# Retention and low-rank mixer kernel: queries four tokens to a partition, a reordered start, u^T of the first group by matmul, first y2 over w2 blocks

## The chip, the cores and the metric

One core of one Trainium2 chip. The metric is the device time of one execution in microseconds, as the median of several executions. Kernels that were timed together ran on the same chip, in turns with the kernel before.

## The reference

```python
# q, k, v: [8, 8, 576, 64] fp32 (batch, heads, tokens, head size)
scores = q @ k^T / 8
x = (scores * gamma_h ** (i - j) for i >= j, else 0) @ v     # retention, gamma_h = 1 - 2 ** (-5 - h)
x = x as [8, 576, 512]
u = x + (x^T @ U @ V)^T          # U: [576, 32], V: [32, 576]: mixes tokens
out = u + relu(u @ w_ch1) @ w_ch2  # 512 -> 2048 -> 512
```

## The kernel before

Two batches make a pair of 9 chunks of 128 tokens; chunk 4 ("X") holds the last 64 tokens of one batch and the first 64 of the other. The work goes in 8 groups (one per batch, of 4 or 5 chunks). A *front* computes attention and mixer of a group: k and q are transposed, `psc` are the scores, `ret` the masked scores, `po` the attention output, `xt` its scaled form, `psa`/`a_sb` the product with U, `ph` the product with V, `ut` = u, `uT` = u transposed. The MLP of a group is y1 = relu(u w1), then y2 = y1 w2, then `o_sb` = y2 + u, which is stored. While group g's MLP runs on PE, group g+1's front is woven in between, and group g+2 is loaded.

```python
    def load_chunk(p, c):                    # one token to a partition, 256 B runs
        t = qkv_pool.tile([P, 3, H, D], BF16, tag="qkv", name="qkv")
        f = stage.tile([P, 3, H, D], FP32, tag="stage", name="stage_t")
        for j, dram in ((1, k), (0, q), (2, v)):
            for rows, b, t0 in parts(p, c):
                nc.sync.dma_start(out=f[rows, j, :, :],
                    in_=dram[b, :, t0:t0 + L, :].rearrange("h s d -> s h d"))
        # ... casts; v is scaled on gpsimd

        def T(c):                            # q and k of a chunk in one transpose
            if not pe_transpose:
                nc.sync.dma_start_transpose(
                    out=qkT, in_=t[:, 0:2, :, :].rearrange("p j h d -> p (j h d)"))
                return                       # (the first group: on PE)

        def MT(c):
            if not pe_transpose:
                nc.sync.dma_start_transpose(out=dst, in_=st["u", c])
                return

        def Y2(i, f0):
            # ... 16 matmuls over f into one PSUM tile, then:
                nc.vector.tensor_tensor(out=o_sb, in0=ps, in1=st["u", c0 + i], op=ALU.add)
                nc.sync.dma_start(
                    out=out_flat[row0 + i * P:row0 + (i + 1) * P, :], in_=o_sb)

    # ...
        for c in A_CH:                       # chunks 0 to 4 of the first pair
            load_chunk(0, c)
            if c == 1:
                load_mixer()
            if c == 3:
                load_w1([0])
        interleave([], front_items(0, [], True, 0))
        load_w1(range(1, dff // W1B))
        load_w2()
        for a in chunks_of(1):
            load_chunk(*a)
        for g in range(2 * NP):
            main = mlp_items(g // 2, g % 2, sts[g // 2])
            fill = front_items(g + 1, chunks_of(g + 2)) if g + 1 < 2 * NP else []
            interleave(main, fill, 0.35 if g == 0 else 0.05, 0.9)
```

All transposes by DMA, all loads of q, k, v and all stores are issued by SyncE (SP) in this order of the program; `w1`, `w2`, U and V are loaded from GpSimd (POOL).

## Time and profile before

| | before |
|---|---|
| time, median (range) | 382.49 us (377.34 to 382.87) |
| span of the profiled run, granted clock | 381.3 us, 0.978 |
| PE busy | 329.2 us, 86% |
| first y1 matmul of groups 0, 1, 2 | 41.8, 93.0, 142.9 us |
| output store, issue to landing | 2.2 us |
| uT transpose, issue to landing | 2.5 us |

The page of the profile: busy time of each engine, then digits for 40 equal slices of the span (9 is 90% or more).

```profile
span 381.3 us, 5987 instructions
PE 329.2 (86%) x2440; PEld 176.1 (46%) x2440; DVE 142.9 (37%) x199; ACT 123.2 (32%) x244; POOL 62.4 (16%) x86
PE   2655794887997999999998989998999999999995
PEclk9999996799899999999999999999999999999999
```

The line `PEclk` is the clock that PE was granted, in tenths of full speed. After the first quarter PE is busy nearly all the time. What is left to win is at the start. A group boundary is the other place to watch. Here is the one between groups 2 and 3, SP's queue and then PE, with start, duration, what, and in brackets how long the engine had been idle and for what.

```profile
175.32 0.39 SPq L444 DMA_DIRECT2D out_dram<-o_sb  x1
175.77 2.54 SPq L390 DMA_TRANSPOSE uT<-ut  x2
178.99 0.34 SPq L444 DMA_DIRECT2D out_dram<-o_sb  x1
179.39 2.66 SPq L214 DMA_TRANSPOSE qkT<-qkv  x2
```

The busy time by stretches, during the last group, where nothing else moves data. The columns are the stretch, its length, the busy us of PE, of its weight loads (PEld), of DVE, ACT and POOL (each with its number of instructions), the granted clock, the DMA share (the mean busy share of the 16 DMA engines) and GB/s.

```profile
365.00:366.00 1.00, 1.00 (x6) 0.47 (x5) 0.00 (x0) 0.00 (x0) 0.00 (x0) 1.00 0.67 262
366.00:367.00 1.00, 1.00 (x7) 0.41 (x6) 0.02 (x1) 0.00 (x0) 0.00 (x0) 1.00 0.00 0
```

The last store is issued 3.2 us before the span ends.

### The profile page before, as it was taken

How to read it: one execution, taken by the hardware profiler on the slowest of the kernel's cores; microseconds unless marked ns; L12 is line 12 of the kernel's file. 1: busy time of each engine (PE TensorE's matmuls, PEld its weight loads, DVE VectorE, ACT ScalarE, POOL GpSimd, SP SyncE). 2: the span in 40 equal slices, each digit the busy share in tenths (PEclk: the TensorE clock that was granted, in tenths of full speed). 3: DMA queues.
4: the chain of work that ended last, by engine and by line, in shares of the span. 5: the costliest groups of instructions: out<-in, count | busy, mean ns of one | idle time of the engine just before them, and what ended most of it. 6: DMA issues, size and time to landing. Idle time of an engine off the chain costs nothing.

```text
span 381.3 us, 5987 instructions
## 1 busy us (share of the span) xinstructions
PE 329.2 (86%) x2440; PEld 176.1 (46%) x2440; DVE 142.9 (37%) x199; ACT 123.2 (32%) x244; POOL 62.4 (16%) x86
## 2 busy tenths in 40 slices
PE   2655794887997999999998989998999999999995
PEld 1432341433673444544664435444764445447642
DVE  4454201555252342544335324552544424340021
ACT  3322361200572006501771035303660056007600
POOL 2746821221022000121021001220121000000000
PEclk9999996799899999999999999999999999999999
DMA  9999999995995149995994279997991480040012
GB/s 181 206 210 179 199 196 186 206 185 132 191 212 97 57 110 194 202 211 136 175 228 83 73 126 218 186 173 157 218 196 40 114 153 2 28 125 29 0 57 83
DMA packets 173659, 54.81 MB, mean 144 GB/s; under 512 B 164864, under 2 KB 169024, under 8 KB 173632
## 3 DMA queue, kind: packets, MB, share of 16 engines
q1 hardware_dynamic: 167840, 50.09, 73.6%
q0 software_dynamic: 5792, 4.34, 7.5%
q8 instruction: 19, 0.31, 0.4%
q14 instruction: 8, 0.07, 0.1%
HBM read 37.00 MB, written 9.44 MB: 122 GB/s over the span
## 4 chain that ended last, share of the span: by engine, by line
PE 56%; DMA 18%; SPq 13%; DVE 6%; issue 3%; ACT 2%; POOL 1%; DVEq 0%; POOLq 0%
DMA stage_t<-in_q_dram 8%; SPq L190 7%; DMA uT<-ut 4%; SPq L214 4%; DMA stage_t<-in_v_dram 3%; DVE ret L281 3%; PE po L294 2%; PE psc L254 2%; PE psa L361 2%; PE ph L379 1%; SPq L390 1%; DVE o_sb L443 1%; DVE qkv L194 1%; DMA qkT<-qkv 1%; DMA U_A<-in_moe_U_dram 1%
## 5 line engine op out<-in xcount | busy, mean ns | idle before, releaser
L426 PEld LDWEIGHTS <-w_sb 128*128 128x128 bf16 x768 | 72.2, 100 | 55.9 <-issue 17.3
L195 POOL TENSOR_TENSOR qkv<-stage_t,vscale 128x512 bf16<-128x512 f32 x36 | 38.1, 1060 | 216.2 <-DMA stage_t<-in_v_dram 156.0
L281 DVE TENSOR_TENSOR ret<-psc,tri 128x1024 bf16<-128x1024 f32 x32 | 39.1, 1223 | 50.9 <-PE psc L254 50.9
L194 DVE CAST qkv<-stage_t 128x1024 bf16<-128x1024 f32 x36 | 25.8, 718 | 64.4 <-DMA stage_t<-in_q_dram 64.4
L300 DVE TENSOR_TENSOR xt<-po,qscale 128x512 bf16<-128x512 f32 x36 | 24.8, 689 | 17.6 <-PE po L294 17.5
L366 ACT ACTIVATE a_sb<-psa 128x512 bf16<-128x512 f32 x8 | 4.8, 597 | 80.5 <-PE psa L361 76.5
L385 DVE TENSOR_TENSOR ut<-ph,xt 128x512 bf16<-128x512 f32 x36 | 24.6, 689 | 14.5 <-PE ph L379 14.4
L294 PE MATMUL po<-qkv,ret 128*128 128x64 bf16 x288 | 15.6, 201 | 9.6 <-DVE ret L281 9.6
L254 PE MATMUL psc<-qkT 64*128 64x128 bf16 x288 | 16.0, 238 | 8.8 <-DMA qkT<-qkv 5.7
L294 PEld LDWEIGHTS <-ret 128*128 128x128 bf16 x288 | 13.5, 103 | 19.6 <-DVE ret L281 15.1
L244 ACT ACTIVATE s_sb<-pss 128x512 bf16<-128x512 f32 x32 | 19.0, 593 | 5.4 <-PE pss L237 5.4
L254 PEld LDWEIGHTS <-qkT 64*128 64x128 bf16 x288 | 9.1, 102 | 22.3 <-issue 10.1
L237 PEld LDWEIGHTS <-qkv 128*128 128x128 bf16 x128 | 10.5, 105 | 6.9 <-issue 1.9
L237 PE MATMUL pss<-qkv 128*128 128x128 bf16 x112 | 12.0, 235 | 1.8 <-ACT s_sb L244 1.0
L437 PEld LDWEIGHTS <-y_3686 128*128 128x128 bf16 x80 | 7.8, 98 | 9.3
L437 PEld LDWEIGHTS <-y_929 128*128 128x128 bf16 x80 | 7.8, 101 | 9.3 <-issue 1.1
L437 PEld LDWEIGHTS <-y_1861 128*128 128x128 bf16 x80 | 7.6, 98 | 8.6
L437 PEld LDWEIGHTS <-y_2793 128*128 128x128 bf16 x80 | 7.6, 98 | 8.6
L221 PE MATMUL pst<-ident,qkv 128*128 128x128 bf16 x40 | 5.2, 311 | 7.3 <-DVE qkv L194 7.3
L226 ACT ACTIVATE qkT<-pst 128x1024 bf16<-128x1024 bf16 x5 | 5.1, 1024 | 15.1 <-PE pst L221 15.1
L163 POOL DMA_DIRECT2D w_sb<-in_moe_w_ch_dram x16 | 9.3, 597 | 3.5 <-DMA w_sb<-in_moe_w_ch_dram 3.5
L437 PEld LDWEIGHTS <-y_1457 128*128 128x128 bf16 x64 | 6.1, 98 | 7.1
(522 smaller groups left out, 536.7 us busy)
## 6 DMA issues: line engine op xcount, KB each, us to landing
out_dram<-o_sb SPq DMA_DIRECT2D x36, 256.0 KB, 2.2
stage_t<-in_k_dram SPq DMA_DIRECT2D x32, 256.0 KB, 3.9
stage_t<-in_q_dram SPq DMA_DIRECT2D x32, 256.0 KB, 5.1
stage_t<-in_v_dram SPq DMA_DIRECT2D x32, 256.0 KB, 5.1
w_sb<-in_moe_w_ch_dram POOLq DMA_DIRECT2D x16, 128.0 KB, 7.2
w_sb<-in_moe_w_ch_dram POOLq DMA_DIRECT2D x8, 256.0 KB, 11.5
stage_t<-in_k_dram SPq DMA_DIRECT2D x8, 128.0 KB, 4.8
stage_t<-in_q_dram SPq DMA_DIRECT2D x8, 128.0 KB, 4.8
```

What stands on the lines that cost most here:

```text
L190: nc.sync.dma_start(out=f[rows, j, :, :], in_=dram[b, :, t0:t0 + L, :].rearrange("h s d -> s h d"),)
L194: nc.vector.tensor_copy(out=t[:, 0:2, :, :], in_=f[:, 0:2, :, :])
L195: nc.gpsimd.tensor_tensor(out=t[:, 2, :, :], in0=f[:, 2, :, :], in1=vscale[:, c, :, None].to_broadcast([P, H, D]), op=ALU.mult,)
L237: nc.tensor.matmul(pss[:, hp, :], t[:, 1, 2 * hp:2 * hp + 2, :].rearrange("p h d -> p (h d)"), vt[:, 2 * hp:2 * hp + 2, :].rearrange("p h ...
L244: nc.scalar.activation(out=s_sb, in_=pss, func=AF.Copy)
L254: nc.tensor.matmul(psc[:, hl, hp, :], qkT[pb:pb + HALF, NHP + hp, :], qkT[pb:pb + HALF, hp, :], start=True, stop=True,)
L281: nc.vector.tensor_tensor(out=ret.rearrange("p (hp hl) i -> p hl hp i", hl=2), in0=psc, in1=mask[:, None, None, :].to_broadcast([P, 2, NHP ...
L294: nc.tensor.matmul(po[:, hl, hp * D:(hp + 1) * D], ret[:, h, :], t[:, 2, h, :], start=(c == 0 and hp == 0), stop=True, skip_group_check=True,)
L300: nc.vector.tensor_tensor(out=xt.rearrange("p (hp hl d) -> p hl hp d", hl=2, d=D), in0=po[:, :, 0:NHP * D].rearrange("p hl (hp d) -> p hl ...
L385: nc.vector.tensor_tensor(out=ut, in0=ph, in1=st["x", c], op=ALU.add)
L426: nc.tensor.matmul(ps[:, 0:n], w1_sb[:, cc, f * P:(f + 1) * P], uT[:, cc, t0:t0 + n], start=(cc == 0), stop=(cc == NCC - 1),)
L437: nc.tensor.matmul(ps, st["y1"][:, f, i * P:(i + 1) * P], w2_sb[:, f, :], start=(f == 0), stop=(f == NF - 1),)
```

## The change

Its intent: (1) load q in 1 KB runs instead of 256 B, by putting four neighbouring tokens of a head into one partition. The transpose of such a tile gives the tokens of a chunk in permuted order, partition j*32+p holding token 4p+j; the mask, the scales, U, V and the output rows are permuted to match. (2) Give the start an order: batch 0, then w1, then batch 1, then w2, each waiting for the one before. (3) The first group's u^T straight from x and a_sb by matmul, without u. (4) Group 0's y2 over w2 blocks as they land, three chunks at a time. Group 1's front is transposed on PE as well.

```diff
 def load_q(g, quick=False):
+    i = nc.sync.dma_start(out=f,
+        in_=q[g, :, t0:t0 + 4 * P, :].rearrange("h (p j) d -> p h j d", j=J))   # J = 4
 ...
-    nc.sync.dma_start_transpose(out=qkT, in_=<q and k of one chunk>)
+    for m in range(4):                                  # TQ: all four chunks of q
+        nc.sync.dma_start_transpose(
+            out=qT[:, m].rearrange("p hp (j i) -> p (hp j) i", j=J),
+            in_=t[m * PJ:(m + 1) * PJ].rearrange("p hp j hl d -> p (hp j hl d)"))
+    nc.sync.dma_start_transpose(out=kT, in_=<k of one chunk>)    # TK
 ...
 def load_mixer():
+    for t, t0, m0 in ((U_A, 0, 0), (U_B, HALF, 1)):
+        for j in range(J):                              # 11 small loads in place of 6 (8 here)
+            nc.gpsimd.dma_start(out=t[j * PJ:(j + 1) * PJ, m0:m0 + 4, 0:R], in_=src[j])
+    ... put_v(V_A, 0, 0)                                # V rows permuted by a DVE copy
 ...
 Y2:
-    nc.sync.dma_start(out=out_flat[row0 + i * P:row0 + (i + 1) * P, :], in_=o_sb)
+    nc.sync.dma_start(out=dst.rearrange("(p j) d -> j p d", j=J), in_=o_sb)
 ...
+    load_x(0, 0)
+    w1_last = load_w1()
+    first = first_front()                               # u^T = x^T + (V^T a)^T in PSUM
+    i = load_q(1)
+    tc.add_manual_dep(i.ins, w1_last.ins.name, SYNC)    # batch 1 after w1
+    ... load_w2() after two chunks of batch 1 ...
+            if g == 0:
+                fill = [MH of group 0] + Front(1, True).items([], x_alone=True)
+                interleave(mlp.y1_items(), fill, 0.3, 1.2)
+                i = load_q(2)
+                tc.add_manual_dep(i.ins, w2_last.ins.name, SYNC)
+                ...
+                for f in range(NF):
+                    for i in range(3):
+                        mlp.Y2(i, f, 1)
+                mlp.Y2(3, 0, NF)
+                continue
```

## The prediction

> What bounds it now. PE is busy 329 of 381 us (busy table), and from 120 us on 18.3 to 19.4 of each 20 us (busy time by stretches): the later groups are bound by PE. The loss is at the start: the timeline has the first y1 matmul at 41.8 us and the second group's y1 at 93.0; the 288 us after that lose about 13 us to short waits (uT transposes 0.6 to 1.9 us each, waits view). Between 41.8 and 93, PE stands 4.65 us for a transpose stuck behind loads and then runs cold (630 ns a matmul against 379). DMA moves 180 to 210 GB/s, nearly all packets under 512 B: batches 0 and 1, w1 and w2 compete.
>
> What the change does.
> 1. Queries, a third of the loads, in 1 KB runs (256 B before). The Trainium skill, "DMA: Bandwidth & Descriptors", Specifications, gives 512 B as the least for line rate; at the trace's 190 GB/s for 256 B runs a group's q (1 MB) takes 5.5 us, now an estimated 3.5.
> 2. Batch 0 alone, then w1 (issued after the last V scaling, about 21 us, landed by about 34), then batch 1, then w2.
> 3. First front: per chunk about 3.8 us in place of 4.7 (0.6 less each in transposes and copy); u^T in one piece replaces four 1.8 us rounds of ph, ut, pu, uT. Against it: twelve small mixer loads on POOL (0.55 us each) before the second V scaling, and V rows copied by DVE ahead of the second mask. First y1 at 36 to 39 us.
> 4. Group 1's front is transposed on PE, with a tail of five rounds (1.5 to 1.8 us) that y1 no longer fills, then 64 y2 matmuls (13.8 us). Second y1: about 88 us, 5 earlier; the second group gains 3 more, having no uT wait.
> 5. Later groups: four q transposes and one of k before the first scores; before, one. An issue takes SP 1.2 us (128x512) or 1.25 (128x1024), landing 2.5 after. They start after the previous group's last output, about 0.5 us after y1 starts; the scores stand 3.5 to 3.9 us into PE's order. Landing after 6 to 9 us: a wait of 2 to 5 us in groups 2 to 6.
> 6. Outputs have 4 as slowest dimension. The same page ("Why a DMA increments its semaphore by 16") would put them on 4 engines: 256 KB in an estimated 2.4 us, delaying uT transposes behind them by about 1 us and the tail by 1 to 2. The trace has 2.2 us to landing now.
>
> Sum: -8 (start), -3 (second group), +1 to +5 in each of five groups, +1.5 (tail): 376 to 398. If transposes of 32 partitions issue faster, or the start gains more, it is a gain of 10 to 20. I settle at 382.
>
> Predicted: 382 us, 8 in 10 between 362 and 402; faster by over 2% 0.35, within 2% 0.32, slower by over 2% 0.33.
>
> Signs. First y1 at 36 to 39 us (step 3 too pessimistic if under 32); second y1 at 84 to 91. Waits view: PE at a group's first psc for DMA kT or qT, 2 to 5 us (none: step 5 wrong). uT waits above 1.9 us, outputs landing after more than 2.2 us (step 6). q landing in well under twice a k load's time per byte (step 1).
>
> What would make it wrong: q's transposes being cheap; front 1 hidden better behind y1; four-engine outputs holding up loads.

## More of the kernel before

```profile
178.07 0.71 PE L426 MATMUL ps_y_1862<-uT,w_sb 128*128 128x320 bf16 x4
179.72 0.70 PE L426 MATMUL ps_y_1868<-uT,w_sb 128*128 128x320 bf16 x4 [0.94 <-DMA uT<-ut]
182.80 0.40 PE L254 MATMUL psc<-qkT 64*128 64x128 bf16 x8
```

(`SPq` is SP's queue, and the duration of its lines is the time that SP took to issue; `x2` means two in a row; `DMA_DIRECT2D` is a plain copy by DMA.) SP alternates stores, uT transposes of the group that is about to start, and the q and k transposes of the first two chunks of the front after it. PE waits 0.94 us for the last uT, and not at all for the scores (`psc`), which stand some 3 us further on in its order.

## The result, and the profile after

The changed kernel is right and takes 449.26 us median (448.0 to 452.81, 4 runs) against 381.66 us for the kernel before. Ratio 1.181, 95% interval 1.169 to 1.193. (Ratios here are the mean time of one kernel's fast runs over that of the other's fast runs of the same rounds, so they are not quite the ratio of the medians quoted.)

| | before | after |
|---|---|---|
| span, granted clock | 381.3 us, 0.978 | 448.1 us, 0.914 |
| first y1 of group 0 | 41.8 | 41.6 |
| of group 1 | 93.0 | 100.4 |
| of group 2 | 142.9 | 158.3 |
| from there to the end | 238.4 | 289.8 |

So the loss of 66.8 us is 7.4 us in the start, 8.0 us in group 1, and 51.4 us in groups 2 to 7. The page of the profile after:

```profile
span 448.1 us, 6172 instructions
PE 350.1 (78%) x2486; PEld 188.1 (42%) x2520; DVE 157.6 (35%) x249; ACT 129.6 (29%) x257; POOL 66.4 (15%) x103
PE   2357787797789669985999569974999489959993
PEclk9999999598899979997799888996899979997997
```

PE has a hole at each group boundary, and its clock is below full after each hole. The same boundary as above, between groups 2 and 3, SP and then PE:

```profile
196.47 0.54 SPq L607 DMA_DIRECT2D out_dram<-o_sb  x1
197.06 4.01 SPq L504 DMA_TRANSPOSE uT<-ut  x2
201.17 0.54 SPq L607 DMA_DIRECT2D out_dram<-o_sb  x1
201.80 7.35 SPq L318 DMA_TRANSPOSE qT<-q_bf  x4
209.20 1.26 SPq L342 DMA_TRANSPOSE kT<-kv  x1
```

```profile
199.03 0.72 PE L581 MATMUL ps_y_2039<-uT,w_sb 128*128 128x320 bf16 x4
204.12 1.23 PE L581 MATMUL ps_y_2045<-uT,w_sb 128*128 128x320 bf16 x4 [4.37 <-DMA uT<-ut]
211.74 0.61 PE L403 MATMUL psc<-qT,kT 64*128 64x128 bf16 x8 [2.88 <-DMA kT<-kv]
```

Two uT transposes take SP 4.01 us where they took 2.54; the last uT comes 4.37 us late where it was 0.94; then four transposes of q take 7.35 us, and the scores wait 2.88 us more. After the first wait the first three y1 sets take 1.23 us for four matmuls against 0.71 before it: PE is at half clock. The Trainium skill, "TensorE: Matmul & The Clock Gate", Part 1, says that the clock falls to half when PE is idle and takes about 3.4 us of work to come back. The trace agrees the first time, and not in length the second. In stretches of 1 us the granted clock is 0.50 from 205 to 207 us and back at 1.00 at 208, some 3.4 us after PE began again at 204.1; after the second wait it is 0.50 from 211 to 217, and comes back in the stretch after, some 6 us after PE began again at 211.7.

Some of the waits of PE over the whole run (who waited for whom: total us, times, longest), first of before, then of after; the other lines, some as long, are left out:

```profile
PE po L294 <- DVE ret L281: 9.6, 10, 2.6
PE psc L254 <- DMA qkT<-qkv: 5.7, 2, 4.6
PE ps_y_936 L426 <- DMA uT<-ut: 1.9, 1, 1.9
PE ps_y_2800 L426 <- DMA uT<-ut: 1.6, 1, 1.6
```

```profile
PE psc L403 <- DMA kT<-kv: 14.3, 6, 3.3
PE po L440 <- DVE ret L428: 10.1, 7, 3.9
PE ps_y_2575 L581 <- DMA uT<-ut: 6.6, 1, 6.6
PE ps_y_3523 L581 <- DMA uT<-ut: 6.6, 1, 6.6
PE ps_y_3899 L581 <- DMA uT<-ut: 5.2, 1, 5.2
```

In all, the uT tile's own view gives 8.1 us in 8 waits before and 32.5 us in 6 waits after.

What are the transposes behind? After group 0's y2, three stores are issued at once, with the loads long done. The chain of waits and the busy time by stretches of the changed kernel:

```profile
96.95 6.31 DMA out_dram<-o_sb
103.39 0.70 DVE o_sb L599
```

```profile
102.00:103.00 1.00, 0.00 (x0) 0.00 (x0) 0.00 (x0) 0.15 (x1) 0.00 (x0) 1.00 0.27 104
103.00:104.00 1.00, 0.00 (x0) 0.00 (x0) 0.61 (x1) 0.00 (x0) 0.00 (x0) 1.00 0.26 100
```

The chain lists 6.31 us for the stores, and the next `o_sb`, for which only three buffers exist, is made after that; the first columns of the stretches show PE doing nothing. The DMA share stands at about a quarter at 100 GB/s: 4 of 16 engines work. That agrees with the Trainium skill, "DMA: Bandwidth & Descriptors", "Why a DMA increments its semaphore by 16 and not by 1", which says that a transfer uses the largest number of engines up to 16 that divides the slowest dimension of both sides. The changed store has `j` (4) as slowest dimension. How long one such store moves data is seen best at the end, where it is alone: the last one moves from 443.0 to 446.5 us, 3.5 us in place of 0.9. From its issue to the end of the span it is 7.0 us, where it was 3.2.

### The profile page after: what moved, and what is told of

Read it like the earlier page. It is cut to its first block, busy times and chain, and to the rows that moved or that the text cites. A ratio compares the mean times of both kernels' runs of the same rounds, so it can differ in the third digit from the quotient of the medians.

```text
span 448.1 us, 6172 instructions
## 1 busy us (share of the span) xinstructions
PE 350.1 (78%) x2486; PEld 188.1 (42%) x2520; DVE 157.6 (35%) x249; ACT 129.6 (29%) x257; POOL 66.4 (15%) x103
## 4 chain that ended last, share of the span: by engine, by line
PE 58%; DMA 14%; SPq 14%; DVE 7%; issue 2%; ACT 2%; POOL 1%; DVEq 0%; POOLq 0%
SPq L318 8%; SPq L504 4%; DMA kv_f<-in_k_dram 3%; DMA q_f<-in_q_dram 3%; DMA kT<-kv 3%; PE psc L403 2%; PE po L440 2%; DMA uT<-ut 2%; PE psa L469 2%; PE ph L486 2%; DMA out_dram<-o_sb 1%; DVE ret L428 1%; DMA kv_f<-in_v_dram 1%; DVE ut L492 1%; DVE o_sb L599 1%
## 5 line engine op out<-in xcount | busy, mean ns | idle before, releaser
L581 PEld LDWEIGHTS <-w_sb 128*128 128x128 bf16 x768 | 77.9, 108 | 93.3 <-issue 29.5
L244 POOL TENSOR_TENSOR kv<-kv_f,vscale 128x512 bf16<-128x512 f32 x32 | 33.5, 1051 | 252.6 <-DMA kv_f<-in_v_dram 162.5
L448 DVE TENSOR_TENSOR xt<-po,qscale 128x512 bf16<-128x512 f32 (+1 forms) x37 | 25.5, 690 | 24.1 <-PE po L440 24.0
L403 PE MATMUL psc<-qT,kT 64*128 64x128 bf16 x256 | 14.0, 235 | 14.8 <-DMA kT<-kv 14.3
L440 PE MATMUL po<-kv,ret 128*128 128x64 bf16 x256 | 14.1, 202 | 8.8 <-DVE ret L428 8.8
L259 DVE CAST kv<-kv_f 128x512 bf16<-128x512 f32 x32 | 15.3, 482 | 12.2 <-DMA kv_f<-in_k_dram 10.9
L403 PEld LDWEIGHTS <-kT 64*128 64x128 bf16 x256 | 7.9, 100 | 25.3 <-DMA kT<-kv 17.2
L382 PE MATMUL pss<-kv 128*128 128x128 bf16 x112 | 12.1, 236 | 6.9 <-POOL kv L244 6.8
L238 DVE CAST q_bf<-q_f 128x512 bf16<-128x512 f32 x30 | 11.6, 450 | 13.6 <-DMA q_f<-in_q_dram 13.6
L382 PEld LDWEIGHTS <-kv 128*128 128x128 bf16 x112 | 9.4, 108 | 10.9 <-issue 7.7
```

The source lines that it names most:

```text
L244: nc.gpsimd.tensor_tensor(out=dst[rows], in0=src[rows], in1=vscale[rows, c, :, None].to_broadcast([n, H, D]), op=ALU.mult,)
L382: nc.tensor.matmul(pss[:, hp, :], pair_cols(st["k", c], hp), pair_cols(vt, hp), start=(first and hp == 0), stop=True, skip_group_check=True,)
L403: nc.tensor.matmul(psc[0:n, hl, hp, 0:n], kT[pb:pb + HALF, hp, 0:n], qTv[pb:pb + HALF, hp, 0:n], start=True, stop=True,)
L440: nc.tensor.matmul(po[0:n, hl, hp * D:(hp + 1) * D], ret[:, h, 0:n], vt[:, h, :], start=((c == 0 or not cross) and hp == 0), stop=True, sk ...
L448: nc.vector.tensor_tensor(out=st["x", c][rows].rearrange("p (hp hl d) -> p hl hp d", hl=2, d=D), in0=po[rows, :, 0:NHP * D].rearrange("p h ...
L581: nc.tensor.matmul(ps[:, 0:n], w1_sb[:, cc, f * P:(f + 1) * P], uT[:, cc, t0:t0 + n], start=(cc == 0), stop=(cc == NCC - 1),)
```

## The experiments

At each boundary two things of the change come together: the stores run on four engines, and the q transposes of the next front stand behind the last store. The first theory (A) was that the stores are the main cost; the rival (B), that it is the late, fourfold q transposes; a third (C), that the new start and the new order of work cost something by themselves. The first six variants start from the changed kernel, then three from the kernel before, and the last four build a better version. Times are medians, given with the kernel before on the same chip.

### e1: stores on 16 engines

```diff
-    nc.sync.dma_start(out=dst.rearrange("(p j) d -> j p d", j=J), in_=o_sb)
+    nc.sync.dma_start(out=dst, in_=o_sb)
```

The rows come out in the wrong order: only the address pattern differs.

> Outputs written in plain row order (wrong rows on purpose, same bytes, 2 KB runs), nothing else changed: the output's slowest dimension is 128 again and not 4. Theory A (outputs run on 4 of 16 engines, about 100 GB/s, and the uT and qT transposes queue behind them): DMA share while outputs run is no longer capped at 0.25, uT waits at group starts fall from 4.4 to 6.6 us back to 1 to 2, the 4 qT issues fall from 7.7 to about 5 us; time 395 to 412 us from 449. Rival B (the five transposes before the first scores are the cost, whatever the outputs do): uT waits stay, time 435 us or more.

Measured: 418.42 us against 380.33 (ratio 1.097, 1.090 to 1.104). The signs of A came, but not its time of 395 to 412 us: more remains than A had room for. A stretch of 1 us in which three stores are out at once, and the waits of PE for transposes:

```profile
99.00:100.00 1.00, 1.00 (x6) 0.48 (x5) 0.29 (x1) 0.00 (x0) 0.00 (x0) 1.00 1.00 369
```

```profile
PE psc L403 <- DMA kT<-kv: 26.0, 7, 5.5
PE ps_y L581 <- DMA uT<-ut: 5.3, 6, 1.4
```

The same data leave at 369 GB/s, with all engines at work (share 1.00), and the uT waits are as small as before the change. But the wait for the scores' transposes has grown from 14.3 to 26.0 us: what the uT no longer lose, the q transposes do. So the stores cost 31 us net here, and a second loss was hidden behind the first.

### e2: q transposes ahead of the stores

```diff
+    def ahead(self): self.TQ(); self.TK(5 * self.par)   # q, first k of the front after next,
+    # called in the middle of the front before it, not at its start
-    add(0, self.TQ); add(0, self.TK, main[0])           # at the start of a front
```

> The four q transposes and the first k transpose of the next front are issued one group earlier (ahead of the MA stage of the front before), outputs still on 4 engines. Theory A: the waits for kT at the first psc (31 us PE and PE-load together) go, but the uT waits of 4 to 7 us stay or grow; 425 to 440 us. Rival B: most of the loss goes; 395 to 415 us.

Measured: 451.06 us against 380.33 (1.186, 1.179 to 1.192), result correct. No gain at all, against 10 to 25 us expected. PE's waits for transposes are now one line:

```profile
PE ps_y L588 <- DMA uT<-ut: 51.4, 8, 11.7
```

The wait for kT is gone, as intended, and the wait for uT has grown from 32.5 to 51.4 us. Part of that is the edit's own: the five transposes moved ahead now stand before the uT transposes in SP's queue, between the stores, and with fast stores (e10 against e1) the same move raises the wait for uT from 5.3 to 11.8 us. While the stores crawl, it matters little which transpose stands behind them.

### e4: plain stores, plain q, new start

```diff
-    load_q: one load of 1 KB runs; U, V, mask permuted; stores permuted
+    f[:, m] <- q[g, :, t0 + m*P : +P, :].rearrange("h s d -> s h d")   # 4 loads; U, V, mask, stores plain
```

The new start, the order of loads, u^T by matmul and the late q transposes (four of 128 x 512) stay.

> The query layout undone (one token to a partition, 256 B runs, plain outputs, plain U and V loads); DMA order, first u^T by matmul, first y2 over w2 blocks and four separate q transposes of 128x512 stay. If the layout alone (through its outputs) made the loss in later groups: groups 2 to 7 as in before plus the wait for five transposes, in all 395 to 415 us. If the new start and order are to blame for more than about 15 us: over 415 us. If q in 1 KB runs is worth something, the start is 2 to 4 us later than in the changed kernel.

Measured: 416.06 us against 380.33 (1.094, 1.090 to 1.098), result correct. That is about e1 again (418), a little slower than expected, with the same line of waits, 26.0 us in 7 for kT. So 1 KB loads of q, the eleven mixer loads and the V copies, taken together, cost and gain next to nothing over the whole run; what remains in e1 is theory B and possibly C. By its expectation 416 lies just in the branch that blames the new start for more than 15 us; e7 below shows that it is mostly B. The first y1 came at 35.7 us in place of 41.6, and still the second came at 100.3: the six microseconds gained in the first front did not pass on.

### e8: the same permuted rows in four stores of 32 partitions

```diff
-    nc.sync.dma_start(out=dst.rearrange("(p j) d -> j p d", j=J), in_=o_sb)
+    rows = dst.rearrange("(p j) d -> j p d", j=J)
+    for j in range(J):
+        nc.sync.dma_start(out=rows[j], in_=o_sb[j * PJ:(j + 1) * PJ])
```

> Right results: each permuted output in four DMAs of 32 partitions, whose slowest dimension is 32 on both sides. Theory A: all 16 engines work, as the run with plain outputs but with 4 issues of about 0.35 to 0.5 us where one was: 400 to 418 us. If a small DMA of 32 partitions still goes to few engines, little is gained: 430 us or more.

Measured: 434.01 us against 380.33 (1.142, 1.138 to 1.146), result correct. A repair of less than the expected size; 434 lies in the branch that was written for stores that still go to few engines, so it has to be seen which it is. The busy time in the stores' stretch, and SP's queue:

```profile
101.00:102.00 1.00, 1.00 (x9) 0.60 (x7) 0.00 (x0) 0.65 (x3) 0.00 (x0) 1.00 0.52 131
```

```profile
192.31 1.94 SPq L609 DMA_DIRECT2D out_dram<-o_sb  x4
```

The DMA share is about a half, at 131 GB/s. SP takes 1.94 us to issue the four stores of one tile, and 256 KB in 1.94 us are 135 GB/s: the stores now go as fast as SP can issue them. The trace speaks against few engines: in the 0.1 us from 102.6 us the small stores move 307 GB/s, above the 100 of four engines, so the mean is low because of the gaps between issues. PE still waits 19.4 us for uT and 23.6 for kT.

### e7 and e10: both losses removed

e7 is e4 with e2's edit; e10 is e1 with e2's edit.

> Natural query layout (as e4_qnat, 416 us) with the first transposes of the next front issued one group earlier (as e2_tqearly). If outputs on 4 engines and the five late transposes are two separate losses, the psc waits for kT (26 us in e4_qnat) go now that no output stands in the way: 383 to 393 us. If the wait only moves to the uT transposes, as in e2_tqearly: 408 us or more.

> Four-token query layout, plain outputs (wrong rows on purpose), early transposes: the same as e7_qnat_early but for the query layout. If 1 KB query runs are worth something: 2 to 8 us under e7_qnat_early. If they are worth nothing where loads are not the limit: within 4 us of it, or a few us over it for its later start (41.0 against 35.7 us for the first y1).

Measured: e7 388.2 us (1.022, 1.017 to 1.028; correct), e10 391.77 us (1.031, 1.024 to 1.038; wrong rows), both against 380.62. e7 came in the middle of its range, 383 to 393. Now the changed layout makes a table of two by two:

| stores | q transposes late | q transposes early |
|---|---|---|
| on 4 engines (changed kernel, e2) | 449.3 | 451.1 |
| on 16 engines (e1, e10) | 418.4 | 391.8 |

Repairing the transposes is worth nothing while the stores are slow, and 27 us when they are fast. Repairing the stores is worth 31 us while the transposes are late, and 59 when they are early. The two losses share a queue, and each hides part of the other, so neither single removal gives its size. Of the changed kernel's 67.6 us (449.26 less 381.66), both together take away 57.5. (The entries come from three sessions; the kernel before had 381.7, 380.3 and 380.6 us in them.) Most of the rest is in the start: the first y1 of group 2 is 6.5 us later in e10 than before (149.4 against 142.9), and from there to the end it takes 242.0 us, e7 239.5, and the kernel before 238.4. No gain from the 1 KB runs of q is to be seen, 391.8 us in e10 against 388.2 in e7, though e10 also has the eleven mixer loads and the V copies to carry.

### b1, b2, b3: the kernel before with its stores on 4, 8 and 16 engines

```diff
-    nc.sync.dma_start(out=rows, in_=o_sb)
+    nc.sync.dma_start(out=rows.rearrange("(p j) d -> j p d", j=4), in_=o_sb)   # b2: j=8, b3: j=16
```

This is the disputed cost on its own: no new start, no q transposes. All three have wrong rows. b3 is the control: its rows are permuted and scattered too (by 16 and not by 4), but its slowest dimension is 16. It was made because b1 alone could not tell the number of engines from the order of the rows.

> The kernel before with only its outputs permuted (row order wrong on purpose), so that the slowest dimension is 4. Theory A: that alone costs what it gave back in e1_out16, about 31 us: uT waits of 4 to 6 us at group starts, 405 to 425 us. If the outputs only hurt together with the five transposes: under 395 us.

> As b1_out4 (437 us, rows in wrong order on purpose) with a slowest dimension of 8 instead of 4. If the number of engines is what the slowest dimension sets: outputs at about 200 GB/s and DMA share 0.5, and well under half of the 56 us of b1_out4 (the part over what the transposes can wait): 385 to 405 us. If the permuted row addresses are the cost: about 437 us, as with 4.

> The same with a slowest dimension of 16. If engines: all 16 work, outputs land in about 2.2 us, time within 2 us of before (379 to 383 us) although the rows are permuted. If the permuted row addresses are the cost: 430 us or more.

Measured: b1 436.7 us against 380.62 (1.151, 1.143 to 1.159), b2 404.14 against 381.96 (1.054, 1.042 to 1.065), b3 384.35 against 381.96 (1.009, 1.001 to 1.017). b1 lost more than expected (405 to 425); b2 came in its range of 385 to 405, and b3 some 1 us above its 379 to 383, with stores that land after 2.9 us and not the 2.2 expected. The stretch of 1 us in which the last group stores, in b1, b2 and b3 (share and GB/s are the last two columns):

```profile
421.00:422.00 1.00, 1.00 (x6) 0.49 (x5) 0.00 (x0) 0.00 (x0) 0.00 (x0) 1.00 0.26 100
387.00:388.00 1.00, 1.00 (x7) 0.41 (x6) 0.69 (x1) 0.00 (x0) 0.00 (x0) 1.00 0.45 166
371.00:372.00 1.00, 1.00 (x7) 0.46 (x5) 0.00 (x0) 0.00 (x0) 0.00 (x0) 1.00 0.88 223
```

PE's wait for uT in the three:

```profile
PE ps_y L426 <- DMA uT<-ut: 51.1, 7, 9.7
```

```profile
PE ps_y L426 <- DMA uT<-ut: 22.1, 8, 4.3
```

```profile
PE ps_y L426 <- DMA uT<-ut: 11.5, 8, 1.9
```

One word in an address pattern costs 56 us, and the cost falls with the number of engines: 56, 22, 2 us. Permuted rows as such, which b3 has too, cost at most some 2 us. The time lost is the wait of PE for uT (51.1 us in b1 against 8.1 before the edit) and a clock that falls in the holes: 0.916 granted in b1 against 0.978, and PE busy 339.8 us against 329.2. Together the longer wait (43 us) and the longer busy time (10.6) are 54 of the 57 us by which the span of b1 is longer than before (438.1 against 381.3). One thing these runs leave open: whether the transposes wait because SP's queue is held up by the stores before them, or because the same DMA engines are still busy. No run issues the stores from another engine.

### e9: y2 of group 0 spread over the tail of front 1

e7 still has its second y1 at 101.5 us. In the changed kernel front 1's tail runs alone from 73.6 to 84.2 us, and y2 of group 0 after it, from 84.2 to 100.4, its first nine matmuls at 430 ns each and the later ones at 216. So e9 is e7 with y2, by pairs of chunks over w2 blocks, mixed into front 1, and with batch 2's loads in the middle of it.

```diff
-    interleave(mlp.y1_items(), fill, 0.3, 1.2)     # then y2 by itself
+    interleave(mlp.y1_items() + y2, fill, 0.2, 0.9)
```

> e7_qnat_early with group 0's y2 run two chunks at a time over w2 blocks and spread through front 1, so that y2 fills the tail of five ph, ut, pu, uT rounds. If that tail (73 to 84 us, PE mostly waiting) and the cold y2 after it are what makes the second y1 start at 100 us: it starts at 86 to 92 and the time is 8 to 13 us under e7_qnat_early. If w2 or batch 1 are late anyway: within 4 us of it.

Measured: 382.64 us against 380.62 (1.010, 1.001 to 1.018), result correct. The second y1 came at 83.1 us, 18.4 earlier, but the kernel gained only 5.6. PE's waits in e9:

```profile
PE psc L396 <- DMA kT<-kv: 8.9, 2, 8.6
PE ps_y L581 <- DMA uT<-ut: 11.4, 7, 3.2
```

There is a new wait of 8.6 us for a k transpose: in SP's queue it stands behind batch 2's loads (issued from 71 to 90 us), two stores and four q transposes. Of the 18.4 us, 7.0 are left at the first y1 of group 2 (139.6 against 146.6).

### e11, e12, e13: batch 2 earlier, and the loads not held back

e11 puts batch 2 at the head of y2, transposes q chunk by chunk next to k, and issues the next front's first transposes before the last stores. e12 is e11 without the rule that batch 1 waits for w1; e13 also drops the rule that batch 2 waits for w2.

```diff
-    tc.add_manual_dep(i.ins, w1_last.ins.name, SYNC)     # e12, e13
-    tc.add_manual_dep(i.ins, w2_last.ins.name, SYNC)     # e13 only
```

> e9_mixed with the q transposes chunk by chunk (only the first chunk's q and k transposes ahead, 2 issues of 1.2 us in place of 5), and batch 2's loads and these two transposes put ahead of group 0's outputs in SP's order. If the 8.6 us wait for kT in the second group of e9_mixed came from SP standing behind outputs: it goes, the uT waits fall from 11 to about 8 us in all, and the time is 370 to 377 us. If batch 2's data are late anyway: 379 to 383 us.

> e11_chunk without batch 1's wait for w1. If that wait only leaves DMA idle (share 0.54 in 20 to 30 us): batch 1 is in 4 to 8 us earlier and the second y1 starts 3 to 6 us earlier: 366 to 374 us. If w1 is then starved by batch 1 and y1 of group 0 waits for it: no gain, or slower by 2 to 5 us.

> e12_now1 without batch 2's wait for w2 as well. If DMA has room: 0 to 3 us under e12_now1. If batch 2 takes bandwidth from w2 while y2 of group 0 runs over w2 blocks: 2 to 6 us over it.

Measured against 381.15 us: e11 379.42 (0.995, 0.992 to 0.999), e12 372.65 (0.979, 0.975 to 0.983), e13 372.95 (0.978, 0.973 to 0.983), all correct. e11 was expected at 370 to 377 if SP's order was the cause, and 379 to 383 if batch 2's data were late; it came in the second. In its trace the wait of 8.6 us is gone, but batch 2's loads are issued only at 68.2 us, after w2, and PE waits 6.5 us from 65.9 us for DVE, which itself waits for batch 2's q; the second y1 went back from 83.1 to 91.5. e12 came in its range of 366 to 374. e13 came without the gain of 0 to 3 us that it might have had; e12 and e13 agree within their ranges: the second rule costs nothing that can be seen here. The first costs 6.8 us. Busy time from 20 to 30 us, e11 and then e12:

```profile
20.00:30.00 10.00, 7.49 (x95) 5.03 (x94) 6.94 (x9) 2.55 (x5) 8.03 (x14) 1.00 0.73 96
```

```profile
20.00:30.00 10.00, 7.51 (x96) 5.05 (x94) 6.43 (x10) 2.55 (x5) 6.90 (x12) 1.00 1.21 197
```

PE does the same work in both, but with the rule the DMA moves 96 GB/s, and without it 197: batch 1 could have been coming in. Not all of the 6.8 us need be that: without the rule w2 is also issued from 45.1 us in place of 52.9, batch 2's loads from 59.9 in place of 68.2, and the wait of 6.5 us is gone. The second y1 moves from 91.5 to 86.0 us, and the third from 140.3 to 132.6. e12 is 2.2% under the kernel before by the medians (by the ratio's interval it is surely faster, but whether by 2% is open), and 17% under the changed one (372.65 against 449.26); its page, against those shown above:

```profile
span 370.0 us, 6216 instructions
PE   2577889779997979999999989999989999999995
```

Groups 2 to 7 take 237.4 us in it, as in the kernel before (238.4). The gain is in the start: the third y1 comes at 132.6 us, where it was 142.9.

## Why the prediction was wrong

The prediction was 382 us, 362 to 402; the measured time is 449. The step that failed is step 6: its mechanism, four engines and transposes that wait behind the stores, was right, and the term "about 1 us" for the delay of uT (with "1 to 2" for the tail) was mis-sized. In its place PE waits 32.5 us in all for uT where it waited 8.1, and the same stores alone cost 56 us (b1).

- **Step 6, the stores.** "would put them on 4 engines: 256 KB in an estimated 2.4 us, delaying uT transposes behind them by about 1 us and the tail by 1 to 2." The engines were right: share about 0.25 at 100 GB/s. One store took somewhat longer, about 3.5 us where it is alone at the end. The delay was far off: single waits for uT last up to 6.6 us, and the tail, from the last store's issue to the end of the span, is 3.8 us longer (7.0 against 3.2). The delay was reckoned as that of one transpose behind one store. The trace has stores two or three at a time, transposes between them, SP's issue slowed with them (4.01 us for two uT in place of 2.54), the next output waiting for a buffer, and a cold clock after each hole. Alone it costs 56 us on the kernel before (b1), and 31 or 59 here, by what else is repaired. The signs "uT waits above 1.9 us" and "outputs landing after more than 2.2 us" came (the page after gives no landing times of stores; the 3.5 us and the tail show it), and the prediction's last line, "four-engine outputs holding up loads", was close: they held up transposes.
- **Step 5, the q transposes.** "a wait of 2 to 5 us in groups 2 to 6": 14.3 us in 6 waits in the changed kernel, up to 3.3 each; 26.0 us in 7 in e1; worth 27 us once the stores are fast. The mechanism and the size of a wait hold (in e1 up to 5.5). The sum "+1 to +5 in each of five groups" missed that steps 5 and 6 use the same queue, and the hope that transposes of 32 partitions issue faster failed: the shortest issue is 1.20 us for 32 x 2048 (e8), 1.19 for 128 x 512, 1.25 for 128 x 1024.
- **Step 3, the first front.** "First y1 at 36 to 39 us": 41.6. The small loads (eleven, not the twelve of the text) kept POOL until 18.45 us, with about 0.55 us each as estimated. But the copy of V's rows by DVE, which was named and not costed, took 3.50 us for the first half and 0.41 for the second, of the same shape. With it, POOL's work in that time:

```profile
19.28 3.50 DVE L173 COPY V_A<-V_nat 32x512 bf16<-32x512 bf16 x1 [3.77 <-DMA V_nat<-in_moe_V_dram]
22.79 0.41 DVE L173 COPY V_B<-V_nat 32x512 bf16<-32x512 bf16 x1
18.45 3.05 POOL L244 TENSOR_TENSOR kv<-kv_f,vscale 128x512 bf16<-128x512 f32 x3
```

  POOL goes on with a fourth multiplication until 22.49, and the copy ends 0.3 us after it. It is so in all five kernels with permuted V (changed kernel, e1, e2, e8, e10: 3.50 to 3.77 us). In e4, e7, e9 and e11 to e13, where the copy is made in a gap of POOL's, it takes 0.28. The times say that DVE stood for POOL; no run moves the copy to test it. e4, with V loaded in natural order, has its first y1 at 35.7. Of these 5.9 us the small loads are worth most: they put the second V scaling, and with it PE's work on the second chunk, off by 3.8 us (19.56 against 15.72), and the copy comes on top.
- **Step 4, the second front.** "Second y1: about 88 us": 100.4. The tail took 10.6 us and y2 after it 16.2 in place of 13.8, as PE was cold in between, and both began late. "The second group gains 3 more": from the second to the third y1 it took 57.9 us in place of 49.9, with group 0's slow stores and the first of step 5's waits inside. e9 shows where most of it can be had back: mixed with the front, y2 lets the second y1 come at 83.1.
- **Step 2, the order.** The loads went in the order described. The load that waits for w1 was issued at 38.9 us, so w1 may have landed later than the predicted 34, and the order was taken for a gain. Holding batch 1 back for w1 costs 6.8 us (e11 to e12).
- **Step 1, the runs of 1 KB.** Small, as part of the sum allowed: at the start q is in by 6.44 us, when its first cast begins, where in natural order (e4) the casts begin from 4.08 to 7.77 as the pieces land. The sign held: in e1 1 MB of q lands in 5.8 us, and 256 KB of k in 5.1 (medians). In the whole no gain is to be seen: e10 is no faster than e7.

Open is how the 3.6 us between e7 and e10 come about (the later first y1, from the small loads and the V copy, is one candidate), and by which way the stores hold up the transposes, SP's queue or the engines.

## What to carry to other kernels

Read the slowest dimension of a store's address pattern before you permute rows in it: 4 in place of 128 put a store on a quarter of the DMA engines. A slow transfer costs what waits behind it, so list what else is issued behind it in that moment, and do not cost it as a single delay. Where two losses stand in one queue, remove each, and then both: here the same repair was worth 0 or 27 us, depending on the other. And before you make one load wait for another, look whether the DMA is full in the meantime: here it was not, and the rule cost 6.8 us.

## What the Trainium skill lacked or had wrong

- "DMA: Bandwidth & Descriptors", "Why a DMA increments its semaphore by 16 and not by 1": its rule for the number of engines held (slowest dimension 4: share 0.26, 100 GB/s; 128: share 1.00, 369 GB/s). It says nothing of its cost: 56, 22 and 2 us in this kernel for 4, 8 and 16 engines, of the first two 43 and 14 us by longer waits for transposes that stand behind the stores.
- The same page has no time for the issue of a transpose from SBUF to SBUF on this chip by its shape. Here the shortest issues took SP 1.19 us (128 x 512), 1.25 us (128 x 1024) and 1.20 us (32 x 2048), so four small ones cost four times one large one; behind slow stores the median uT issue rose from 1.22 to 1.77 us.
- The same page does not give an issue time for stores on this chip by their pattern. Here the median for 256 KB was 0.36 us plain, and 0.54, 0.60 and 0.55 with a slowest dimension of 4, 8 and 16 (b1, b2, b3); four of 64 KB took SP 1.94 us (e8).
- The same page, Specifications, gives 512 B as the least for line rate. No run here shows a gain from it in the time: with q in 1 KB runs the kernel is no faster (391.8 against 388.2 us), though no run has that difference alone.
